# Finished weights and transposed rows as plane and exponential buffers, row-by-row guards, a reordered prologue and a new order of work in an attention and token-MLP kernel

## The chip, the cores and the metric

The kernel runs on one core of a Trainium2 chip. The core has a matrix engine (TensorE, PE in the profile, with its weight loads as PEld), a vector engine (VectorE, DVE), an activation engine (ScalarE, ACT), a general engine (GpSimd, POOL) and a queue engine (SyncE, SP) from which most transfers are issued. The metric is the device time of one execution in microseconds, as the median of several runs.

## The reference

For an input `x` of 2048 rows and 512 columns in bf16:

```python
xn = _layernorm(x)
def _A_ref(x, wqkv, wo):                     # 32 heads of 16 columns
    qkv = (x @ wqkv).reshape(B, S, 3, H, Dh)...
    p = _softmax(einsum("bhqd,bhkd->bhqk", q, k) * Dh ** -0.5)
    return einsum("bhqk,bhkd->bhqd", p, v)... @ wo
def _B_ref(x, w1, b1, w2, b2):               # an MLP over the rows, F = 1376
    h = _layernorm(x)
    u = _gelu(einsum("bsd,sf->bdf", h, w1) + b1)
    return (einsum("bdf,fs->bds", u, w2) + b2)...
return x + _A_ref(xn, ...) + _B_ref(xn, ...)
```

There are 32 heads x 2048 x 2048 exponentials to take, which is by far the largest part of the elementwise work.

## The kernel before

**Score tiles.** Attention is cut into 32 blocks: four groups of 512 queries (`qb`), each with eight groups of four heads. Within a block four heads sit in four rows (`r`, 32 partitions each) of PE, and the keys are cut into 16 tiles of 128 (`kt`). One unit is a tile of 128 keys by 512 queries for one head: 64 units a block, 2048 in all. The position in the order of work, `pos()`, is counted in blocks of 64 units. A score matmul (`score_mm`, L629) writes a unit into one of seven PSUM banks; the eighth collects P times V (`pv_mm`, L655).

**Two ways to an exponential.** An "A" unit is taken by ACT (`exp_tile`, L642): one, two or three banks in one instruction, written into the ring `pT` of `NU` = 16 slots, and then one PV matmul. A "D" unit is taken by VectorE (`dve_first`, L675): it adds a bias, clips and rounds the score to int16, whose bits read as bf16 are a piecewise linear power of two. Two more such numbers, shifted by constants, correct it. Four D units lie side by side in one plane of 2048 columns, and `make_plane` (L684, an addition of a constant to packed 64-bit integers on POOL; L686 on VectorE) makes the two shifted planes from the first. Each of the three is multiplied by V (the first by a scaled copy, `V17b`), so a D unit takes three PV matmuls.

**Planes.** `planes` holds `NXP` = 5 of them. The memory of `x_sb` gives four more once all 16 row tiles are normalized, that of `xn_sb` four more once the first MLP layer (`ut`) is done: `free_planes` (L1242). In those eight, each write of a row (L675) or of a whole plane (L684) also writes the keys of the old tenant (`plane_alias`), so the planner sees two writes to different rows of such a plane as writes of the same memory and puts a wait between them.

**Order of work.** The program is written out by a planner that runs while the kernel is built: `Sched` keeps each engine's stream, durations and dependences and turns a dependence on another operation into a semaphore wait. A prologue (L702 to L735) is in a fixed order: statistics, logarithm and exponential for the inverse deviation (`ln_rstd`, L508 and L510, on ACT), normalization (L515), transposes on PE (L554), copies out of PSUM (L566 and L567), the first Q and K, and the masked Q of the first two blocks (L593 and L595). After that a loop picks, for the engine that is free first, the best of what is ready: `burst` chooses how many of up to four scores go to ACT and how many to VectorE, and "chains" (K, V and Q projections, the MLP's two layers, output projection, epilogues) fill PE between them. Some 36 settings steer the choice; `STEP_VALUES` has one row of them for each block of 64 units. Those that matter below are `d_from` (position from which D units may be taken), `bal` and `bal_w` (tolerance for VectorE ending after ACT and the weight of what is over it) and `d_keep` and `d_last` (the last key tiles that are kept for ACT).

**Weights.** `wqkv_sb` holds the Q, K and V weights with 1536 columns for each of four slices of the contraction, and `xnT` the transposed normalized rows, 2048 columns for each slice. K and V of all heads are made in the first blocks, Q of a group of heads just ahead of its block. `w2blk` takes two blocks of the second MLP weights; `chain_late` loads the first two of them soon after the first block, though the second layer begins near position 15.7.

Of the kernel before, what the change touches and what calls it, by code (L numbers as in the profile page):

```python
# [41 lines left out]
def _plane_sum(i):  # L42
# [15 lines left out]
NXP = 5  # L58
DEBUG_CHAINS = False
# [1822 lines left out]
```

## Time and profile before

| | us |
|---|---|
| median of 3 runs | 688.4 (687.91 to 689.09) |
| profiled execution | 683.5 |
| its span, first to last instruction | 681.7 |
| ACT busy | 665.6 |
| PE busy | 661.3 |
| DVE busy | 572.3 |
| POOL busy | 481.5 |

The granted TensorE clock was 1.00 throughout. A group of instructions in the profile is one source line with one pair of tiles; its columns are the count, the busy time, the mean duration of one in nanoseconds, and the idle time of the engine ahead of the group with what ended it. Durations of neighbours on one engine can overlap, so the sum over a group may be above the time that the engine was occupied. A window of the trace lists for each engine the busy time and the number of instructions.

### The profile page before, as it was taken

The page shows a single profiled execution, that of the slowest core. Times are in us where ns is not written, and L with a number is a line of the kernel's source. Part 1 is how long each engine was busy: PE and PEld are TensorE (multiplying, and loading weights), DVE is VectorE, ACT ScalarE, POOL GpSimd, SP SyncE. Part 2 cuts the span into 40 slices and gives each one's busy share as a digit, 9 for nine tenths or more (in the row PEclk, how much of TensorE's full clock was granted, in tenths as well). Part 3 has the DMA queues.
Part 4 walks back from the last instruction along what each step waited for, and adds up shares of the span by engine and source line. Part 5 has one row for each costly group of instructions (what it writes and reads, how often), then busy time and mean ns, then how long its engine had stood idle before and what let it go on. Part 6 is the DMA issues. An engine that isn't in the chain of part 4 may idle for free.

```text
span 681.7 us, 20346 instructions
## 1 busy us (share of the span) xinstructions
PE 661.3 (97%) x8598; PEld 202.1 (30%) x8598; DVE 572.3 (84%) x937; ACT 665.6 (98%) x810; POOL 481.5 (71%) x506
## 2 busy tenths in 40 slices
PE   8899999999999999999999999999999999999997
PEld 3444433222222222222222222222222223222322
DVE  7987887778978888888898888888889888988875
ACT  6999999999999999999999999999999999999995
POOL 2407677887656866576896885776867898887783
PEclk9999999999999999999999999999999999999999
DMA  7033000201112111220103202121122112111001
GB/s 216 4 63 92 19 19 8 61 19 33 48 41 57 36 32 34 45 45 5 32 11 76 54 26 64 31 75 34 28 54 58 41 25 62 39 45 43 19 19 47
DMA packets 69956, 29.99 MB, mean 44 GB/s; under 512 B 56494, under 2 KB 66734, under 8 KB 69866
## 3 DMA queue, kind: packets, MB, share of 16 engines
q1 hardware_dynamic: 69290, 28.18, 16.9%
q8 instruction: 67, 1.10, 0.7%
q10 hardware_dynamic: 576, 0.52, 0.2%
q14 instruction: 23, 0.19, 0.1%
HBM read 22.15 MB, written 2.61 MB: 36 GB/s over the span
## 4 chain that ended last, share of the span: by engine, by line
ACT 82%; PE 12%; DVE 3%; POOL 2%; issue 1%; POOLq 0%; DVEq 0%; ACTq 0%
ACT pT L642 80%; PE ps L629 4%; PE ps L655 4%; PE ps L542 3%; POOL planes L684 1%; DVE x_sb L675 1%; ACT xres L968 1%; PE ps L548 1%; POOL x_sb L684 1%; POOL xn_sb L684 0%; ACT mv L510 0%; DVE xn_sb L515 0%; POOLq L335 0%; ACT mv L508 0%; DVE V17b L616 0%
## 5 line engine op out<-in xcount | busy, mean ns | idle before, releaser
L642 ACT ACTIVATE pT<-ps 128x1024 bf16<-128x1024 f32 (+2 forms) x770 | 653.9, 1098 | 1.0 <-PE ps L629 1.0
L629 PE MATMUL ps<-QT,KT 32*128 32x512 bf16 x2048 | 273.7, 385 | 9.3 <-ACT pT L642 4.6
L675 DVE TENSOR_SCALAR planes<-ps 128x512 int16<-128x512 f32 x289 | 193.0, 686 | 36.6 <-PE ps L629 35.6
L655 PE MATMUL ps<-pT,V 128*32 128x512 bf16 x1407 | 217.9, 387 | 1.1 <-DVE V L567 0.5
L675 DVE TENSOR_SCALAR x_sb<-ps 128x512 int16<-128x512 f32 x202 | 138.0, 687 | 29.3 <-PE ps L629 23.9
L629 PEld LDWEIGHTS ps<-QT,KT 32*128 32x128 bf16 x2048 | 75.0, 91 | 274.2 <-ACT pT L642 230.1
L684 POOL INT64_ADD planes<-x_sb x83 | 87.4, 1062 | 44.9 <-DVE x_sb L675 37.1
L675 DVE TENSOR_SCALAR xn_sb<-ps 128x512 int16<-128x512 f32 x150 | 102.4, 687 | 19.6 <-PE ps L629 15.0
L684 POOL INT64_ADD x_sb<-planes x87 | 90.7, 1047 | 33.3 <-DVE planes L675 20.8
L655 PE MATMUL ps<-planes,V 128*32 128x512 bf16 x562 | 111.4, 385 | 0.6 <-POOL planes L684 0.6
L684 POOL INT64_ADD planes<-planes x82 | 89.0, 1089 | 20.3 <-DVE planes L675 15.7
L655 PE MATMUL ps<-x_sb,V 128*32 128x512 bf16 x522 | 101.5, 385 | 0.0
L684 POOL INT64_ADD x_sb<-x_sb x51 | 56.0, 1101 | 38.9 <-DVE x_sb L675 34.9
L655 PE MATMUL ps<-planes,V17b 128*32 128x512 bf16 x289 | 78.0, 385 | 0.0
L655 PEld LDWEIGHTS ps<-pT,V 128*32 128x32 bf16 x1407 | 53.8, 94 | 68.5 <-issue 57.3
L542 PE MATMUL ps<-gT,w2blk 128*32 128x512 bf16 (+1 forms) x704 | 61.4, 383 | 0.0
L542 PE MATMUL ps<-xn_sb,w1blk 128*32 128x512 bf16 x688 | 57.7, 383 | 0.3 <-DVE qraw L875 0.3
L655 PE MATMUL ps<-x_sb,V17b 128*32 128x512 bf16 x202 | 51.1, 385 | 0.2 <-DVE OT L1096 0.2
L684 POOL INT64_ADD x_sb<-xn_sb x41 | 42.4, 1037 | 12.4 <-DVE xn_sb L675 7.4
L684 POOL INT64_ADD planes<-xn_sb x37 | 39.0, 1059 | 10.3 <-DVE xn_sb L675 7.1
L542 PE MATMUL ps<-xnT,wqkv_sb 128*32 128x512 bf16 (+3 forms) x624 | 43.3, 344 | 2.6 <-DVE xnT L567 1.7
L655 PE MATMUL ps<-xn_sb,V 128*32 128x512 bf16 x198 | 43.9, 385 | 0.0
(86 smaller groups left out, 558.3 us busy)
## 6 DMA issues: line engine op xcount, KB each, us to landing
w1blk<-in_B_w_dram SPq DMA_DIRECT2D x10, 512.0 KB, 4.9
w2blk<-in_B_w_dram SPq DMA_DIRECT2D x16, 320.0 KB, 3.4
denb<-rec_scr SPq DMA_DIRECT2D x16, 256.0 KB
xres<-in_A_x_dram SPq DMA_DIRECT2D x16, 128.0 KB, 3.7
QT<-qraw SPq DMA_DIRECT2D x120, 16.0 KB, 2.4
OT<-OT SPq DMA_DIRECT2D x60, 32.0 KB, 2.0
out_dram<-osb SPq DMA_DIRECT2D x13, 128.0 KB, 1.7
x_sb<-in_A_x_dram SPq DMA_DIRECT2D x2, 512.0 KB
```

The lines of the kernel that those rows point to most:

```text
L542: op = sc.add("pe", lambda e, sl=sl, c=c: e.matmul(dst[sl, :], lhsT=lhsT[:, sl], rhs=rhs, start=start, stop=stop, tile_position=(0, 32 * c ...
L548: return sc.add("pe", lambda e: e.matmul(bank(bk)[:, 0:n], lhsT=zer[:, 512:640], rhs=zer[:, 0:n], start=True, stop=True), reads=[("zer",)] ...
L629: return sc.add("pe", lambda e: e.matmul(bank(bk), lhsT=KT[32 * r:32 * r + 32, T, 128 * kt:128 * (kt + 1)], rhs=QT[32 * r:32 * r + 32, slo ...
L642: return sc.add("act", lambda e: e.activation(pick(pT, us), pick(ps3, bs), ACTF.Exp, scale=EXP_SCALE), reads=[("bank", b) for b in bs], wr ...
L655: return sc.add("pe", lambda e: e.matmul(bank(PV_BANK)[32 * r:32 * r + 32, :], lhsT=vt_[:, off:off + 32], rhs=rhs, start=start, stop=stop, ...
L675: return vec("dve", lambda e: e.tensor_scalar(plane_i[pb][:, 512 * r:512 * (r + 1)], bank(bk), BIAS + SHIFT[0], float(SHIFT[0]), ALU.add, ...
L684: return sc.add("pool", lambda e: e.int64_add(plane_q[pb], plane_q[pb0], -down * LANES), reads=rd, writes=wr, name="plane", occ=1015.0, la ...
L968: return sc.add("act", lambda e: e.activation(gB[0:m, :], gB[0:m, :], ACTF.Tanh, scale=2.0 * GELU_C * GC), reads=kB, writes=kB, occ=t["occ ...
```

## The change

1. **Regions.** `wqkv_sb` is laid out anew with each of the Q, K and V weights in one piece of 2048 columns (`wqkv4`), and `xnT` with each group of 512 rows in one piece (`xnT4`). Planes can now also lie in the first 2048 columns of `w2blk` (until position 14.2), in the V weights (once all K and V are made) and in the transposed rows of the query groups 0 to 2 (once, besides, that group's Q is made). The K weights' piece becomes four more ring slots for exponentials. The x planes come free one by one as four row tiles are normalized.
2. **Guards.** The first use of a region waits for the last operations on its old tenant (`last_ops`, kept in `old_ops`), as extra dependences; a write into a plane now writes the keys of its rows only.
3. **w2.** The first w2 blocks are loaded by a chain of their own from position 14.2, after the last operations on the plane that lay there. A memset of that plane joins the late constants.
4. **Prologue.** Statistics and inverse deviations of tiles 2 and 3 move ahead of copies of earlier tiles, two filling matmuls go, the copy of tile 2 goes to VectorE, the last 128 columns of the first Q go to bank 3, and the masked copies of Q are made in parts of 384 and 128 columns.
5. **Settings.** All 32 rows of `STEP_VALUES` have new numbers.

```diff
+RING_W = 1
+W2_POS = 14.2
...
-    (200.0, 2000.0, 10, 0, 1.2, 4, 4, 60, 0, 6, 0.0, 0, 3.0, 1.0, -0.1, 0.1, 2, 0.2, 2, 0.2, 1500, 2, 60.0, True, 1, False, 5, 4, 0, 1.5, 1000.0, 5, 6, 100.0, False, 3300.0),
...
+    (0.0, 2000.0, 8, 0, 0.8, 4, 2, 60, 0, 4, 400.0, 1, 3.0, 1.0, 0.1, 0.2, 2, 0, 2, 0.1, 800, 2, 100.0, True, 3, False, 5, 3, 0, 1.5, 1400.0, 6, 8, 0.0, False, 3300.0),
...
+        xnT4 = xnT_flat[:, :].rearrange("p (b ct n) -> p b ct n", b=NQB, ct=NCT)
+        wqkv4 = wqkv_flat[:, :].rearrange("p (j ct n) -> p j ct n", j=3, ct=NCT)
...
+            z += [lambda: memset("pool", w2_flat.bitcast(F32)[:, 0:1024], 0.0, [("pl", P_W2, r) for r in range(4)], 900)]
...
+        def qt_evac_part(e_, src, c0, c1, bk, key, eng):
+            rd, wr = [("bank", bk)] + [("qmask", e_, r) for r in range(4)], key
+            if eng == "act":
+                return vec("act", lambda e: e.activation(QT[:, e_, c0:c1], src, ACTF.Identity, scale=qmask[:, e_:e_ + 1]),
+                           rd, wr, c1 - c0)
...
+        regions += [(f, 2048 * j, [(nm, 4 * j + q) for q in range(4)]) for f, nm in ((x_flat, "x"), (xn_flat, "xn"))
+                    for j in range(4)]
+        P_X, P_XN, P_W2 = NXP, NXP + 4, NXP + 8
+        regions.append((w2_flat, 0, []))
+        P_W = len(regions)
+        regions += [(wqkv_flat, 2048 * (1 + j), [("wqkv", 1 + j, T) for T in range(4)]) for j in range(2) if j >= RING_W]
+        P_XT = len(regions)
+        regions += [(xnT_flat, 2048 * qb, [("xnT", 4 * qb + q) for q in range(4)]) for qb in range(3)]
...
+        U_X = NU + 1
+        N_UX = 4 * RING_W
+        pT_x = wqkv_flat[:, 2048:6144].rearrange("p (u n) -> p u n", n=512)
...
+        def region_deps(pb):
+            if regions[pb][2] and pb not in old_ops:
+                old_ops[pb] = last_ops(regions[pb][2])
+            return old_ops.get(pb, ())
...
-                       [("bank", bk)], [("pl", pb, r)] + plane_alias[pb], 512, name="p1")
+                          reads=[("bank", bk)], writes=[("pl", pb, r)], name="p1", extra_deps=region_deps(pb), **T_DVE(512))
...
-            wr = [("pl", pb, r) for r in range(4)] + plane_alias[pb]
+            wr = [("pl", pb, r) for r in range(4)]
...
         zeros(N_ZERO1)
         ln_rstd(1, 2)
+        ln_stats(2)
+        ln_rstd(2, 3)
         transpose_copy(0, 1, TBK[0], "act")
-        ln_stats(2)
         ln_norm(1)
         transpose_pe(1, TBK[1], 0)
         const_v(0, 1)
         pro_q(0)
-        zeros(N_ZERO2)
-        ln_rstd(2, 3)
+        ln_stats(3)
+        ln_rstd(3, 4)
         transpose_copy(1, 1, TBK[1], "act")
-        ln_stats(3)
         ln_norm(2)
         transpose_pe(2, TBK[2], 0)
-        pro_q(1)
-        ln_rstd(3, 4)
-        transpose_copy(2, 1, TBK[2], "act")
+        for ct in range(NCT):
+            kt_mm(0, 0, 1, ct, 2)
         ln_norm(3)
         transpose_pe(3, TBK[3], 0)
+        pro_q(1)
+        transpose_copy(2, 1, TBK[2], "dve")
+        kt_evac(0, 0, 1, 2, "act")
         pro_q(2)
-        for ct in range(NCT):
-            kt_mm(0, 0, 1, ct, 2)
         transpose_copy(3, 1, TBK[3], "dve")
-        kt_evac(0, 0, 1, 2, "act")
-        pro_q(3)
-        qt_evac_masked(0, 0, 0, 4, "dve")
-        qt_evac_masked(0, 0, 1, 4, "act")
+        pro_evac(0, 0, "act")
+        pro_q3()
+        pro_evac(0, 1, "dve")
+        pro_evac(1, 0, "act")
+        pro_evac(1, 1, "dve")
...
+            ch.steps = [Step("sp", yt_next, 600, gate=lambda: pos() >= W2_POS and P_W2 not in pl_busy) for _ in range(NW2)]
...
         def free_planes():
-            lim = list(range(NXP))
-            if nrm_done[0] == NT:
-                lim += list(range(NXP, NXP + 4))
+            lim = list(range(NXP)) + [P_X + j for j in range(4) if nrm_done[0] >= 4 * j + 4]
             if ut_done[0] == NFT:
-                lim += list(range(NXP + 4, NXP + 8))
+                lim += list(range(P_XN, P_XN + 4))
+            if consts_ok[0] and pos() < W2_POS:
+                lim.append(P_W2)
+            if kv_done():
+                lim += list(range(P_W, P_XT)) + [P_XT + q for q in range(3) if q_done[q] == 4]
             return [j for j in lim if j not in pl_busy]
```

More of the change, by code (lines that the diff above doesn't have):

```diff
@@ L574, in kt_mm @@
         def kt_mm(T, t0_, n_, ct, bk, off=0):
-            return mm_full(bank(bk)[:, off:off + 128 * n_], wqkv_sb[:, ct, D + 128 * T: D + 128 * T + 128],
-                           xnT[:, ct, 128 * t0_:128 * (t0_ + n_)], 128, 128 * n_, ct == 0, ct == NCT - 1,
+            return mm_full(bank(bk)[:, off:off + 128 * n_], wqkv4[:, 1, ct, 128 * T: 128 * T + 128],
+                           xnT4[:, t0_ // 4, ct, 128 * (t0_ % 4):128 * (t0_ % 4 + n_)], 128, 128 * n_, ct == 0, ct == NCT - 1,
                            [("wqkv", 1, T)] + [("xnT", t) for t in range(t0_, t0_ + n_)], bk)
@@ L584, in qt_mm @@
             t0_ = 4 * qb + c0 // 128
-            return mm_full(bank(bk)[:, c0:c0 + n], wqkv_sb[:, ct, 128 * T:128 * (T + 1)],
-                           xnT[:, ct, 512 * qb + c0:512 * qb + c0 + n], 128, n, ct == 0, ct == NCT - 1,
+            return mm_full(bank(bk)[:, c0:c0 + n], wqkv4[:, 0, ct, 128 * T:128 * (T + 1)],
+                           xnT4[:, qb, ct, c0:c0 + n], 128, n, ct == 0, ct == NCT - 1,
                            [("wqkv", 0, T)] + [("xnT", t) for t in range(t0_, t0_ + n // 128)], bk)
@@ L596, in qt_evac_masked @@
                        rd, wr, 565)
+        def qt_evac_part(e_, src, c0, c1, bk, key, eng):
[3 more added lines that the diff above has]
+                           rd, wr, c1 - c0)
+            return vec("dve", lambda e: e.tensor_scalar(QT[:, e_, c0:c1], src, qmask[:, e_:e_ + 1], None, ALU.mult),
+                       rd, wr, c1 - c0 + 50)
         def v_mm(t, T0_, T1_, ct, bk, off=0):
             n = 128 * (T1_ - T0_)
-            return mm_full(bank(bk)[:, off:off + n], xnT[:, ct, 128 * t:128 * (t + 1)],
-                           wqkv_sb[:, ct, 2 * D + 128 * T0_:2 * D + 128 * T1_], 128, n, ct == 0, ct == NCT - 1,
+            return mm_full(bank(bk)[:, off:off + n], xnT4[:, t // 4, ct, 128 * (t % 4):128 * (t % 4 + 1)],
+                           wqkv4[:, 2, ct, 128 * T0_:128 * T1_], 128, n, ct == 0, ct == NCT - 1,
                            [("wqkv", 2, T) for T in range(T0_, T1_)] + [("xnT", t)], bk)
@@ L632, in score_mm @@
                 tile_position=(32 * r, 0)),
-                reads=[("KTt", T, kt), ("QT", slot_q, r)], writes=[("bank", bk)], name="sc", cfg="S", n=512, last=last)
+                reads=[("KTt", T, kt), ("QT", slot_q, r)] + ([("QTp", b)] if b < 2 else []), writes=[("bank", bk)], name="sc", cfg="S", n=512, last=last)
         ps3 = ps[:, :].rearrange("p (b n) -> p b n", n=512)
@@ L641, in pick @@
                 return t3[:, v[0]:v[0] + w, :] if w > 1 else t3[:, v[0], :]
-            return sc.add("act", lambda e: e.activation(pick(pT, us), pick(ps3, bs), ACTF.Exp, scale=EXP_SCALE),
-                          reads=[("bank", b) for b in bs], writes=[("pT", u) for u in us], name="exp",
+            return sc.add("act", lambda e: e.activation(slots(us), pick(ps3, bs), ACTF.Exp, scale=EXP_SCALE),
+                          reads=[("bank", b) for b in bs], writes=[("pT", u) for u in us], name="exp", extra_deps=slot_deps(us),
                           occ=427.0 * w + 50.0, lat=427.0 * w + 248.0)
@@ new lines, in bass_parallel_sum__softmax_full_mha__mixer_token_mlp__prompt_kernel, with last_ops @@
+        plane_i = [f.bitcast(I16)[:, o:o + 2048] for f, o, _ in regions]
+        plane_b = [f[:, o:o + 2048] for f, o, _ in regions]
+        plane_q = [f.bitcast(I64)[:, o // 4:o // 4 + 512] for f, o, _ in regions]
+        U_X = NU + 1
+        N_UX = 4 * RING_W
+        pT_x = wqkv_flat[:, 2048:6144].rearrange("p (u n) -> p u n", n=512)
+        old_ops = {}
+        def last_ops(keys):
+            z = {}
+            for k in keys:
+                for o in [sc.last_writer.get(k)] + list(sc.readers.get(k, ())):
+                    if o is not None:
+                        q = ("d", id(o)) if o.is_dma else o.eng
+                        if q not in z or o.pos > z[q].pos:
+                            z[q] = o
+            return list(z.values())
@@ new lines, in region_deps, with slot_deps, slots @@
+        def region_deps(pb):
+            if regions[pb][2] and pb not in old_ops:
+                old_ops[pb] = last_ops(regions[pb][2])
+            return old_ops.get(pb, ())
+        def slot_deps(us):
+            if us[0] >= U_X:
+                if "ring" not in old_ops:
+                    old_ops["ring"] = last_ops([("wqkv", 1 + j, T) for j in range(RING_W) for T in range(4)])
+                return old_ops["ring"]
+            return ()
+        def slots(us):
+            t3, a = (pT_x, us[0] - U_X) if us[0] >= U_X else (pT, us[0])
+            return t3[:, a:a + len(us), :] if len(us) > 1 else t3[:, a, :]
@@ L681, in make_plane @@
             rd = [("pl", pb0, r) for r in range(4)]
[L682 removed]
+            wr = [("pl", pb, r) for r in range(4)]
             if eng == "pool":
                 return sc.add("pool", lambda e: e.int64_add(plane_q[pb], plane_q[pb0], -down * LANES),
[L685 to L687 removed]
+                              reads=rd, writes=wr, name="plane", occ=1015.0, lat=1130.0, port=True, extra_deps=region_deps(pb))
+            return sc.add("dve", lambda e: e.tensor_scalar(plane_i[pb], plane_i[pb0], -float(down), None, ALU.add),
+                          reads=rd, writes=wr, name="plane", port=True, extra_deps=region_deps(pb), **T_DVE(2048, 4.0))
         for i in range(N_ZERO0):
@@ L700, in zeros, with pro_q3, pro_evac @@
                 zero_mm(7)
+        def pro_q3():
+            for ct in range(NCT):
+                mm_full(bank(3)[:, 0:128], wqkv4[:, 0, ct, 0:128], xnT4[:, 0, ct, 384:512], 128, 128, ct == 0, ct == NCT - 1,
+                        [("wqkv", 0, 0), ("xnT", 3)], 3)
+        def pro_evac(e_, c, eng):
+            if c == 0:
+                return qt_evac_part(e_, bank(4)[:, 0:384], 0, 384, 4, [("QTp", e_)], eng)
+            return qt_evac_part(e_, bank(3)[:, 0:128], 384, 512, 3, [("QT", e_, r) for r in range(4)], eng)
         const_q()
@@ L920, in chain_late @@
             steps += [ld_wo] + [lambda e_=e_, r=r: ld_wop(e_, r) for e_ in range(2) for r in range(4)]
-            steps += [lambda: yt_next() for _ in range(NW2)]
             ch = Chain("late", [], 90.0, 0.0, ex=False)
@@ L1286, in ring_pick @@
         def ring_pick(w, taken=()):
-            v = {u: sc.ready(writes=[("pT", u)]) for u in range(NU) if ring_free[u] and u not in taken}
+            v = {u: sc.ready(writes=[("pT", u)]) for u in range(len(ring_free)) if ring_free[u] and u not in taken}
             z = runs_of(v, w)
@@ L1492, in rel @@
                         ring_free[uu] = True
-                    items[u[0]][r].append(dict(t=ex.end, k="A", kt=u[1], rhs=pT[:, uu, :], key=("pT", uu), which=0, rel=rel))
+                    items[u[0]][r].append(dict(t=ex.end, k="A", kt=u[1], rhs=slots((uu,)), key=("pT", uu), which=0, rel=rel))
         def issue_d(ds, i, n):
```

60 lines of the change are left out of this document (32 added, 28 removed), and 62 rows, old and new, of the table STEP_VALUES.

## The prediction

> **What bounds the kernel now.** I read the page's busy shares first, then its chain of work that ended last, then who waited for whom, then the costliest groups.
>
> ```profile
> PE 661.3 (97%) x8598; PEld 202.1 (30%) x8598; DVE 572.3 (84%) x937; ACT 665.6 (98%) x810; POOL 481.5 (71%) x506
> ...
> ACT 82%; PE 12%; DVE 3%; POOL 2%; issue 1%; POOLq 0%; DVEq 0%; ACTq 0%
> ...
> L642 ACT ACTIVATE pT<-ps 128x1024 bf16<-128x1024 f32 (+2 forms) x770 | 653.9, 1098 | 1.0 <-PE ps L629 1.0
> ```
>
> Two engines look full, PE and ACT. The chain is 82% ACT, and the exponentials (L642) sat idle for only 1.0 us. The waits of the whole run say which of the two leads:
>
> ```profile
> PEld ps L629 <- ACT pT L642: 230.1, 535, 0.9
> ```
>
> PE waits for ACT 535 times, 230 us in all (a score cannot start until an exponential has emptied its PSUM bank); ACT's 1.0 us of waiting, in the row above, is its whole wait for PE. So the end is set by ACT's exponentials. The exception is a stretch in which the chain in order of time leaves ACT:
>
> ```profile
> 70.17 0.40 PE ps L629 x4
> ...
> 79.15 0.33 PE ps L655 x4
> ...
> 80.06 0.55 PE ps L655 x8
> ...
> 141.24 0.34 PE ps L629 x2
> 141.60 15.56 ACT pT L642 x15
> ```
>
> From 70 to 141 us it runs mostly on PE. Eight PV matmuls take 0.55 us and four 0.33, so four more cost 0.22, one 0.055.
>
> There are 2048 score tiles of 128x512, and each goes one of two ways: to ACT ("A": one exponential, one PV matmul) or to VectorE ("D": one L675, its share of the plane additions on POOL, three PV matmuls). The whole kernel is one ledger: start to first exponential, the A tiles, tail. So I need the price of an A tile and the D share by stage, from the windows 100 to 340 us (MLP's first layer and gelu running, xn_sb not yet a plane) and 340 to 655 us (xn_sb free). Busy time of all engines, then of L675 alone, then the groups of exponentials in the one window and in the other:
>
> ```profile
> 100.00:340.00 240.00, 236.18 (x2844) 67.53 (x2836) 202.37 (x307) 239.78 (x268) 171.82 (x163) 1.00 0.16 35
> 340.00:655.00 315.00, 312.44 (x3824) 87.00 (x3821) 270.96 (x419) 314.73 (x374) 249.58 (x242) 1.00 0.17 43
> ```
> ```profile
> 100.00:340.00 240.00, 153.44 (x228) 1.00 0.16 35
> 340.00:655.00 315.00, 238.77 (x360) 1.00 0.17 43
> ```
> ```profile
> L642 ACT ACTIVATE pT<-ps 128x1024 bf16<-128x1024 f32 x210 | 204.5, 1216 | 0.2 <-PE ps L629 0.2
> L642 ACT ACTIVATE pT<-ps 128x1536 bf16<-128x1536 f32 x22 | 33.3, 1539 | 0.0
> L642 ACT ACTIVATE pT<-ps 128x512 bf16<-128x512 f32 x25 | 18.6, 819 | 0.0
> ```
> ```profile
> L642 ACT ACTIVATE pT<-ps 128x1024 bf16<-128x1024 f32 x309 | 291.8, 1176 | 0.3 <-PE ps L629 0.2
> L642 ACT ACTIVATE pT<-ps 128x512 bf16<-128x512 f32 x64 | 40.1, 739 | 0.0
> ```
>
> Second window: 618 + 64 = 682 A tiles in 315 us in which ACT did little else, 0.46 us each (durations overlap, so I divide the window). It had 360 D tiles, 34.5% of 1042. First window: 420 + 66 + 25 = 511 A and 228 D, 30.9%. **One tile moved from ACT to VectorE is worth 0.46 us as long as ACT leads.** VectorE is busy 202.4/240 = 84% in the first window and 271/315 = 86% in the second.
>
> **The change part by part.** *Prologue.* ACT and then VectorE in the timeline, 7 to 12 us:
>
> ```profile
> 7.08 0.29 ACT L508 ACTIVATE mv<-mv,epsb 128x1 f32<-128x1 f32 x1
> ...
> 10.09 0.28 ACT L566 ACTIVATE KT<-ps 128x128 bf16<-128x128 f32 x1 [0.95 <-PE ps L542]
> 11.30 0.69 ACT L593 ACTIVATE QT<-ps,qmask 128x512 bf16<-128x512 f32 x1 [0.93 <-DVE QT L595]
> 11.88 0.59 ACT L642 ACTIVATE pT<-ps 128x512 bf16<-128x512 f32 x1
> ```
> ```profile
> 7.02 0.18 DVE L503 BATCH_NORM_AGGREGATE mv<-stats 128x2 f32<-128x6 f32 x1
> ...
> 8.61 0.41 DVE L515 TENSOR_SCALAR xn_sb<-x_sb,mv 128x512 bf16<-128x512 bf16 x1 [0.56 <-ACT mv L510]
> ...
> 10.45 0.75 DVE L595 TENSOR_SCALAR QT<-ps,qmask 128x512 bf16<-128x512 f32 x1 [0.52 <-PE ps L542]
> ```
>
> Tile 3 is normalized (L515, 8.61) behind a wait for ACT, whose logarithms for tiles 2 and 3 stand behind copies of earlier tiles. With logarithm and square root issued ahead of those copies, tile 3's statistics (done at 7.20) pass ACT in about 0.55 us, and its normalization starts near 7.8: 0.8 us earlier. VectorE's order up to there is unchanged, so no load need be earlier. Then the last quarter of Q goes to a bank of its own and VectorE scales 128 columns instead of 512: unseen, between ACT's 0.28 for 128 columns and VectorE's own 0.75; I take 0.3, saving 0.45. ACT scales the other 384 columns twice (between 0.28 and 0.69 each, say 0.55) beside PE's last quarter; its own queue (copy, K, two Q parts) then ends about when the first score does, near 10.6, and is late next. **-1.2 us**, bounds 0 (the following K tiles come no earlier) and -1.3.
>
> *Planes sooner, and more of them.* The first D tile, and the memsets that must precede it:
>
> ```profile
> 45.83 0.69 DVE L675 TENSOR_SCALAR x_sb<-ps 128x512 int16<-128x512 f32 x1
> ```
> ```profile
> 24.57 4.88 POOL L414 MEMSET planes<- 128x1024 f32 x5
> ```
>
> The settings let D begin at 0.8 of a block's 64 tiles; before, row 0 says 1.2 and row 1 (from tile 64) 0.8, so in fact 1.0. That frees 13 tiles; at one in three about 4 become D. The sixth memset costs POOL 4.88/5 = 0.98 us near 30 us, 15 us before it matters. VectorE has layer-norm work there that the planner ranks lower, so I take 3: **-1.4 us**; bounds 0 and -1.8. PE pays 2 x 0.055 = 0.11 us per D tile.
>
> From 100 to 340 us the planner has 9 planes; it gets the w2 block until 14.2 blocks, the V weights once K and V are done, and the transposed rows of finished query blocks: 12, later 13. In the second window it already had 13 and VectorE was only two points busier. If VectorE rises to that 86%, n more D tiles (0.6 us each back to back, below) satisfy 202.4 + 0.6n = 0.86(240 - 0.46n): n = 4. The busiest 20 us of the run bound it above:
>
> ```profile
> 600.00:620.00 20.00, 20.00 (x259) 5.55 (x251) 18.16 (x30) 20.00 (x24) 15.88 (x16) 1.00 0.23 59
> ```
>
> At 18.16/20 = 91%, n = 15. I take 6, near the row that holds for 315 us rather than for 20: **-2.8 us**, bounds 0 and -7.
>
> *Row guards.* In the old code a first write into an x_sb or xn_sb plane also counts as a write of the whole old region, so two rows of one plane wait for each other; in the `planes` tensor they do not. VectorE's timeline near the end:
>
> ```profile
> 658.96 1.28 DVE L675 TENSOR_SCALAR planes<-ps 128x512 int16<-128x512 f32 x2
> 660.16 1.48 DVE L675 TENSOR_SCALAR xn_sb<-ps 128x512 int16<-128x512 f32 x2
> ```
>
> With 0.69 for the last of each, the spacing is 0.59 against 0.79: 0.2 us for each adjoining pair. The groups give the total:
>
> ```profile
> L675 DVE TENSOR_SCALAR planes<-ps 128x512 int16<-128x512 f32 x289 | 193.0, 686 | 36.6 <-PE ps L629 35.6
> ...
> L675 DVE TENSOR_SCALAR x_sb<-ps 128x512 int16<-128x512 f32 x202 | 138.0, 687 | 29.3 <-PE ps L629 23.9
> ...
> L675 DVE TENSOR_SCALAR xn_sb<-ps 128x512 int16<-128x512 f32 x150 | 102.4, 687 | 19.6 <-PE ps L629 15.0
> ```
>
> Idle not put down to PE is 5.4 + 4.6 us against 1.0 for `planes`: about 9 us of VectorE. It is off the path, so worth nothing itself; turned wholly into D tiles it would be 15 x 0.46 = 7 us. After 340 us, where most of it lies and three or four buffers and four exponential slots are also added, I take 3 tiles: **-1.4 us**, bounds 0 and -7.
>
> *At nothing.* The relaid wqkv and xnT keep their column runs, so their matmuls, copies and loads keep their sizes. The two w2 loads move from about 57 us to 14.2 blocks, some 320 us in:
>
> ```profile
> 57.31 1.11 SPq L406 DMA_DIRECT2D w2blk<-in_B_w_dram  x2
> 58.46 0.29 SPq L406 DMA_DIRECT2D w2blk<-in_B_b_dram  x1
> ```
>
> That is six issues, 2.9 us of SP's queue, now waiting for the last readers of that plane. Behind them stand spreads of Q and stores; the spreads are due 1.5 blocks (30 us) ahead, and the first use of w2 is as far off. If a reader were late by a plane's life of some microseconds, that lead covers it.
>
> The Trainium skill, page "SBUF — State Buffer", section "Who interferes with whom", speaks against more D tiles: a VectorE instruction with two SBUF inputs and a GpSimd one that reads SBUF share a port, and one blocks for the other's whole length. The trace agrees:
>
> ```profile
> L959 DVE TENSOR_TENSOR osb<-gT 128x512 f32<-128x512 bf16 (+1 forms) x11 | 11.8, 1076 | 0.1
> ...
> L1096 DVE COPY OT<-ps 128x512 f32<-128x512 f32 x11 | 7.5, 682 | 0.1
> ```
>
> The gelu square takes 1076 ns beside 682 for a copy of that size out of PSUM. Six more D tiles lengthen POOL's 172 us by some 4, 2.5% of an excess of 11 x 0.4 us: 0.1 us. By the rule the sum is -6.7, without it -6.8.
>
> **Sum.** -1.2 - 1.4 - 2.8 - 1.4 = -6.8 us, 12 more D tiles being 5.6 of it. The span goes from 681.7 to 674.9, the profiled execution (683.5, 1.8 around the span) to 676.7. That execution lies 4.9 below the median of the three timed runs (688.4); I apply the difference to the median: **681.6 us**.
>
> **The rivals.** *(a) The new buffers lie idle.* For: VectorE is 84% busy with 9 planes and 86% with 13, so something else (one D tile beside each pair of A tiles, seven PSUM banks) may cap it. Against: the wait between rows is real. Then only prologue and early start are left, -1.2 to -2.6: 686.5. *(b) PE takes over.* Each D tile adds 0.11 us to PE, and between 70 and 141 us PE leads already. Against: in the whole run PE has 230 us of waiting for ACT, so 12 tiles (1.3 us) meet no wall outside that stretch. If half the D gain falls there: -1.2 - 2.8 = -4.0: 684.4. *(c) Slower: the new settings send fewer tiles to VectorE.* The tolerance for VectorE ending after ACT (`bal`) falls from 200 to 0 in the first seven rows and from 900 to 600 in the next ones, which pushes tiles back to ACT at 0.46 us each. For: nothing but the unseen plan stands against it. Against: more planes allow more open groups. With the prologue's -1.2, it decides from 6 fewer D tiles (2.6/0.46), below 635 of now 641; at 12 fewer the time is 688.4 - 1.2 + 5.5 = 692.7.
>
> **How the numbers follow.** Forecast (gain over 4.5 us) 0.66, (a) 0.14, (b) 0.10, (c) 0.10. Faster and slower are told apart from no change at 0.2%, 1.4 us. (a) reaches into "same" with half its chance: faster 0.83, same 0.07, slower 0.10. The range runs from 675.0 (13.4 less: prologue 1.2, early start at its bound of 1.8, and 10.4 of the 14 that bound the other two) to 688.0, leaving out (c) and a little below 675.
>
> **What would show it.** The last exponentials before:
>
> ```profile
> 669.44 4.03 ACT L642 ACTIVATE pT<-ps 128x512 bf16<-128x512 f32 x5
> ```
>
> They end at 673.5, which leaves a tail of 8.2 us. Expected after: first exponential near 10.7 us; first L675 near 40; more than 641 of them, about 653, with the gain in 100 to 340 us; L675 on w2blk, wqkv_sb and xnT; adjoining xn_sb pairs at 1.28 us, not 1.48; w2 loads at 320 us. Wrong: 641 or fewer L675 (a, c); ACT idle before L642 beyond a few us (b); or a tail longer than 8.2 us.

## The result and the profile after

| | before | after |
|---|---|---|
| median of 4 runs | 688.43 (687.91 to 689.09) | 676.13 (675.75 to 677.11) |
| ratio, 95% interval | | 0.9823 (0.9806 to 0.9840) |
| profiled execution, its span | 683.5, 681.7 | 677.1, 675.3 |
| ACT busy | 665.6 | 655.6 |

The change makes the kernel 12.3 us faster, 1.8%. First the page of after: busy time of each engine, the chain that ended last, and the exponentials, which are now L658 and go to the ring `pT` or to the four slots in the memory of the K weights (`wqkv_sb`).

```profile
PE 652.9 (97%) x8608; PEld 202.0 (30%) x8608; DVE 582.0 (86%) x964; ACT 655.6 (97%) x809; POOL 502.6 (74%) x522
...
ACT 84%; PE 11%; DVE 4%; DMA 0%; issue 0%; DVEq 0%
...
L658 ACT ACTIVATE pT<-ps 128x1024 bf16<-128x1024 f32 (+2 forms) x652 | 561.8, 1053 | 4.9 <-PE ps L645 4.6
...
L658 ACT ACTIVATE wqkv_sb<-ps 128x1024 bf16<-128x1024 f32 (+2 forms) x117 | 128.5, 1134 | 0.5 <-PE ps L645 0.5
```

The bound is the same as before: 84% of the chain is ACT. It does 10 us less work, and it waits 5.4 us ahead of its exponentials where the first profile of before had 1.0.

Then the groups of VectorE's first writes (now L721) by the memory that they write: count, least, median and greatest duration, the start of the first and of the last.

```profile
L721 DVE TENSOR_SCALAR planes<-ps x232: 621/681/693, 56.2 to 657.1; 128x512 int16<-128x512 f32 x116
L721 DVE TENSOR_SCALAR x_sb<-ps x182: 627/681/693, 44.1 to 653.4; 128x512 int16<-128x512 f32 x182
L721 DVE TENSOR_SCALAR xn_sb<-ps x102: 628/684/693, 335.2 to 660.7; 128x512 int16<-128x512 f32 x102
L721 DVE TENSOR_SCALAR xnT<-ps x96: 628/681/693, 154.7 to 659.5; 128x512 int16<-128x512 f32 x96
L721 DVE TENSOR_SCALAR wqkv_sb<-ps x33: 674/682/692, 168.9 to 646.9; 128x512 int16<-128x512 f32 x33
L721 DVE TENSOR_SCALAR w2blk<-ps x20: 673/680/692, 70.8 to 293.4; 128x512 int16<-128x512 f32 x20
```

The counts add up to 665 D tiles, 24 more than the 641 of before, and 149 of them (96 + 33 + 20) lie in memory that was not a plane before. The column of first starts tells from when each region is used: w2's block from 71 us, the transposed rows from 155 and the V weights from 169 us, once K and V are done.

The windows in which the prediction worked, for all engines and then for L721 alone:

```profile
100.00:340.00 240.00, 236.51 (x2928) 67.36 (x2926) 213.49 (x328) 239.46 (x279) 197.06 (x181) 1.00 0.17 38
340.00:655.00 315.00, 311.68 (x3880) 89.37 (x3877) 271.53 (x433) 314.92 (x377) 253.00 (x246) 1.00 0.17 44
```
```profile
0.00:100.00 100.00, 24.49 (x37) 0.97 0.24 63
100.00:340.00 240.00, 158.53 (x245) 1.00 0.17 38
340.00:655.00 315.00, 240.26 (x375) 1.00 0.17 44
```

Against before the first window has 17 more D tiles (245 for 228), the second 15 more (375 for 360), the start one fewer (37 for 38) and the end seven fewer (8 for 15), since the kernel now reaches it earlier. VectorE rose from 84% to 89% in the first window (213.5 of 240 us). In the second it stayed at 86%, 271.5 us busy for 271.0, with 15 more tiles: there it is not busier, but does more of the work that counts.

### The profile page after: what moved, and what is told of

It reads as the page before. It is cut to its first block, busy times and chain, and to the rows that moved or that the text cites. A ratio compares the mean times of both kernels' runs of the same rounds, so it can differ in the third digit from the quotient of the medians.

```text
span 675.3 us, 20208 instructions
## 1 busy us (share of the span) xinstructions
PE 652.9 (97%) x8608; PEld 202.0 (30%) x8608; DVE 582.0 (86%) x964; ACT 655.6 (97%) x809; POOL 502.6 (74%) x522
## 4 chain that ended last, share of the span: by engine, by line
ACT 84%; PE 11%; DVE 4%; DMA 0%; issue 0%; DVEq 0%
ACT pT L658 69%; ACT wqkv_sb L658 14%; PE ps L645 4%; PE ps L671 3%; PE ps L549 3%; DVE xn_sb L522 1%; ACT xres L1033 1%; DVE x_sb L721 1%; DVE stats L508 0%; DMA x_sb<-in_A_x_dram 0%; PE ps L561 0%; DVE osb L1024 0%; DVE V L574 0%; ACT L1033 0%; PE ps L1698 0%
## 5 line engine op out<-in xcount | busy, mean ns | idle before, releaser
L658 ACT ACTIVATE pT<-ps 128x1024 bf16<-128x1024 f32 (+2 forms) x652 | 561.8, 1053 | 4.9 <-PE ps L645 4.6
L671 PE MATMUL ps<-pT,V 128*32 128x512 bf16 x1156 | 192.4, 388 | 4.5 <-DVE V L574 4.5
L721 DVE TENSOR_SCALAR planes<-ps 128x512 int16<-128x512 f32 x232 | 153.3, 684 | 25.8 <-PE ps L645 25.3
L721 DVE TENSOR_SCALAR x_sb<-ps 128x512 int16<-128x512 f32 x182 | 120.0, 683 | 14.2 <-PE ps L645 13.6
L658 ACT ACTIVATE wqkv_sb<-ps 128x1024 bf16<-128x1024 f32 (+2 forms) x117 | 128.5, 1134 | 0.5 <-PE ps L645 0.5
L671 PE MATMUL ps<-wqkv_sb,V 128*32 128x512 bf16 x318 | 83.7, 386 | 0.0
L730 POOL INT64_ADD x_sb<-planes x62 | 64.9, 1051 | 21.8 <-DVE planes L721 11.3
L721 DVE TENSOR_SCALAR xn_sb<-ps 128x512 int16<-128x512 f32 x102 | 68.2, 684 | 12.2 <-PE ps L645 11.9
L730 POOL INT64_ADD planes<-x_sb x58 | 62.8, 1088 | 13.9 <-DVE x_sb L721 12.1
L721 DVE TENSOR_SCALAR xnT<-ps 128x512 int16<-128x512 f32 x96 | 63.9, 684 | 9.1 <-PE ps L645 8.8
L730 POOL INT64_ADD planes<-planes x50 | 55.2, 1107 | 7.6 <-DVE planes L721 7.6
```

Source lines behind the costliest of these rows:

```text
L658: return sc.add("act", lambda e: e.activation(slots(us), pick(ps3, bs), ACTF.Exp, scale=EXP_SCALE), reads=[("bank", b) for b in bs], write ...
L671: return sc.add("pe", lambda e: e.matmul(bank(PV_BANK)[32 * r:32 * r + 32, :], lhsT=vt_[:, off:off + 32], rhs=rhs, start=start, stop=stop, ...
L721: return sc.add("dve", lambda e: e.tensor_scalar(plane_i[pb][:, 512 * r:512 * (r + 1)], bank(bk), BIAS + SHIFT[0], float(SHIFT[0]), ALU.ad ...
L730: return sc.add("pool", lambda e: e.int64_add(plane_q[pb], plane_q[pb0], -down * LANES), reads=rd, writes=wr, name="plane", occ=1015.0, la ...
```

## The experiments

Three things were open. The same program of before took 683.5 us in its profile and 688.4 in its timed runs; after waits 5.4 us ahead of its exponentials; and 24 tiles came where 12 were expected, with nothing to tell memory, guards and settings apart. My theory for the first two was that the late memsets on POOL hold VectorE up; for the third that the 9 us of waits between rows, put down as worth little, carry a good part of the gain. The rivals: the 5 us is something that differs all along between executions; and the memory or the settings alone would bring the gain.

**The kernel before once more** (no edit).

> The kernel before, unchanged, to see where its profiled execution (683.5 us) and the median of its timed ones (688.4 us) differ. Theory 1 (the memsets on POOL hold up a normalization L515 on VectorE, by chance 1 us in the profile and 4 to 6 us in most executions): a new profile of about 688 us has a pair of L515 near 27 us that takes 4 us or more instead of 1.6, and ACT idle there. Rival (the clock or the chip): the new profile has the same L515 pair at 1.6 us and is longer everywhere, with a clock below 1.00. Time 688.4 us within 1.

It took 688.17 us (ratio to the other runs of before 0.9999, 0.9990 to 1.0009), and now the profile too is of such an execution, with a span of 686.1. Its timelines on POOL, VectorE and ACT (start, duration, instruction, and in brackets the idle time ahead of it):

```profile
24.08 4.51 POOL L414 MEMSET planes<- 128x1024 f32 x5
28.52 0.20 POOL L414 MEMSET b1r<- 11x128 bf16 x1
28.67 0.95 POOL L414 MEMSET wo_pad<- 128x1024 bf16 x1
```
```profile
25.34 4.37 DVE L616 TENSOR_SCALAR V17b<-V 128x272 bf16<-128x272 bf16 x1
29.62 0.62 DVE L567 COPY xnT<-ps 128x1024 bf16<-128x1024 bf16 x1
```
```profile
31.27 1.57 ACT L642 ACTIVATE pT<-ps 128x512 bf16<-128x512 f32 x3 [3.75 <-PE ps L629]
33.76 1.02 ACT L642 ACTIVATE pT<-ps 128x1024 bf16<-128x1024 f32 x1 [0.91 <-PE ps L629]
```

The scaling of V, 128x272 from SBUF to SBUF, takes 4.37 us and ends as the row of memsets ends (28.67 + 0.95 = 29.62); in the first profile of before it took 0.67. The copy behind it feeds PE, PE feeds ACT, and ACT waits 3.75 and 0.91 us. The place and the sum were expected; the victim was the scaling, not the pair of normalizations.

One sign of the rival appeared too, a clock below 1.00 (0.993 in the mean), but only here: PE ran no matmul from 26 to 30 us, and its granted clock, 1.00 until 28 us, was 0.50 from 30 to 34 us and 1.00 again from 36. The other sign, longer everywhere, did not. Up to the 20th exponential this execution is 0.5 us ahead of the first profile, from the 24th to the last it is 4.3 to 4.4 us behind, so all of the loss arises between them. How much of it is waiting for VectorE and how much the halved clock behind it was not separated; the next run removes both.

**Memsets that let VectorE go first.** The order is kept in both kernels; each memset of the late constants also waits for the last VectorE operation ahead of it in the plan that the kernel marks with `port` (normalizations, scalings of V and the like, from SBUF to SBUF):

```diff
+        last = None
+        for o in sc.order:
+            if o.eng == "dve" and o.port:
+                last = o
+            elif o.eng == "pool" and o.port and o.name == "" and last is not None and last not in o.deps:
+                o.deps.append(last)
         sc.plan()
```

> The kernel before with the same order on every engine; each memset on POOL also waits for the last normalization or other 2x/4x-mode operation on VectorE that stands ahead of it in the planned order. Theory 1: about 684 us, 4 to 5 below the kernel before, and no L515 above 1 us. Rival (the gap between profile and timed runs is elsewhere): 688.4 us, no change.

> The changed kernel with the same order on every engine and the same extra waits of memsets. In its trace a pair of normalizations (L522) takes 4.13 us behind the six plane memsets, and ACT then idles 5.4 us ahead of exponentials instead of 1.0. Theory (the memsets are the cause and ACT's idle time is on the path): 672 us, 4 below the changed kernel, L522 pair at about 0.75 us, idle ahead of exponentials about 1 us. Rival (the K and V projections of that stage are late anyway, PE or VectorE takes the place of the memsets): 675 to 676 us and the idle time stays.

Before with this edit takes 682.96 us (0.9923, 0.9908 to 0.9938): 5.4 us gone, where 4 to 5 were expected. Its POOL and VectorE:

```profile
25.57 0.95 POOL L415 MEMSET planes<- 128x1024 f32 x1 [0.56 <-DVE V17b L617]
26.73 0.95 POOL L415 MEMSET planes<- 128x1024 f32 x1 [0.20 <-DVE xn_sb L516]
```
```profile
25.31 0.20 DVE L617 TENSOR_SCALAR V17b<-V 128x272 bf16<-128x272 bf16 x1
25.43 0.69 DVE L568 COPY xnT<-ps 128x1024 bf16<-128x1024 bf16 x1
26.14 1.68 DVE L516 TENSOR_SCALAR xn_sb<-x_sb,mv 128x512 bf16<-128x512 bf16 x2
```

The scaling is down to 0.20 us, the memsets still end by 31 us, and nobody misses them. The granted clock from 20 to 40 us is 1.00, where the run before this one had 0.83. The span of 681.1 is within 0.6 us of that of the first profile of before.

After with this edit takes 674.19 us (0.9795, 0.9780 to 0.9810), 1.9 below after: the fastest version of this study, 14.2 us below before. That is about half of the 4 us that ACT had waited in this stretch, and it lies between the theory's 672 and the rival's 675 to 676. After's own VectorE and POOL, and then ACT and VectorE with the edit:

```profile
26.95 4.13 DVE L522 TENSOR_SCALAR xn_sb<-x_sb,mv 128x512 bf16<-128x512 bf16 x2 [0.33 <-ACT mv L517]
```
```profile
24.18 4.52 POOL L420 MEMSET planes<- 128x1024 f32 x5
28.63 0.96 POOL L420 MEMSET w2blk<- 128x1024 f32 x1
```
```profile
26.58 5.36 ACT L659 ACTIVATE pT<-ps 128x1024 bf16<-128x1024 f32 x8 [0.51 <-PE ps L646]
31.76 0.35 ACT L516 ACTIVATE mv<-mv,epsb 128x2 f32<-128x2 f32 x1
32.14 0.21 ACT L518 ACTIVATE mv<-mv 128x2 f32<-128x2 f32 x1
...
36.55 1.51 ACT L659 ACTIVATE pT<-ps 128x512 bf16<-128x512 f32 x2 [1.42 <-PE ps L646]
```
```profile
32.38 0.41 DVE L523 TENSOR_SCALAR xn_sb<-x_sb,mv 128x512 bf16<-128x512 bf16 x1 [2.03 <-ACT mv L518]
```

The edit frees the normalizations (4.13 us to 1.57), but the next ones wait 2.03 us for an inverse deviation whose logarithm stands behind eight exponentials in ACT's queue (5.36 us), and ACT then waits 1.42 us for the scores that follow. This second wait belongs to the order of after: before, with the same edit, has six exponentials (3.87 us) ahead of that logarithm, and no such wait.

**The old waits between rows, put back into after.** Same order, same tiles; only each write into a plane of `x_sb` or `xn_sb` waits again for the write into the same plane ahead of it:

```diff
+        last = {}
+        for o in sc.order:
+            if o.reg is not None and P_X <= o.reg < P_W2:
+                d = last.get(o.reg)
+                if d is not None and d not in o.deps:
+                    o.deps.append(d)
+                last[o.reg] = o
         sc.plan()
```

> The changed kernel with the same order on every engine; only the old waits between writes into one plane of x_sb or xn_sb are put back. Theory (VectorE is off the path, the waits cost it 0.2 us for each adjoining pair, some 6 us in all, and ACT hardly notices): 676 to 677.5 us, adjoining xn_sb pairs back at 1.48 us. Rival (a late first write holds a PSUM bank, so PE and ACT get it late): 679 us or more, with more idle time ahead of exponentials.

683.46 us (0.9928, 0.9911 to 0.9944), 7.3 above after: more than half of the whole gain, as the rival had it and not the theory. Of its page, then from the view of L722 alone how long PE's weight loads waited for it (us, times), and the same of L721 in after:

```profile
PE 44%; ACT 41%; DVE 12%; issue 1%; DMA 0%; DVEq 0%
...
L659 ACT ACTIVATE pT<-ps 128x1024 bf16<-128x1024 f32 (+2 forms) x652 | 559.5, 1013 | 8.1 <-PE ps L646 6.5
...
L722 DVE TENSOR_SCALAR x_sb<-ps 128x512 int16<-128x512 f32 x182 | 123.7, 685 | 18.3 <-PE ps L646 12.3
```
```profile
  PEld ps L646: 20.6, 58
```
```profile
  PEld ps L645: 13.4, 35
```

VectorE's idle ahead of `x_sb` writes that is not PE's doing is 6.0 us again (18.3 - 12.3). PE waits 58 times, 20.6 us, for a first write to empty a bank, where in after it waited 35 times, 13.4 us. That 7.2 us more is about what the kernel loses. The chain that ended last, 84% ACT in after, is now 41% ACT and 44% PE. A pair of first writes into `xn_sb` in this run, and one in after:

```profile
400.10 1.47 DVE L722 TENSOR_SCALAR xn_sb<-ps 128x512 int16<-128x512 f32 x2
```
```profile
660.10 1.33 DVE L721 TENSOR_SCALAR xn_sb<-ps 128x512 int16<-128x512 f32 x2
```

The loss builds up over the whole run: the 100th exponential starts 0.3 us later than in after, the 300th 1.8, the 500th 3.9 and the last 7.2. So I read it as the small waits on VectorE reaching PE, and then ACT. The rows agree with that, but no run tests that path by itself, and the edit makes POOL's additions into these planes wait as well.

**The same waits taken away from before.** On top of the memset edit; again the order is kept:

```diff
+        for o in sc.order:
+            if o.reg is not None and o.reg[0] >= NXP:
+                o.deps = [d for d in o.deps if d.reg is None or d.reg[0] != o.reg[0] or d.reg[1] == o.reg[1]]
```

> The kernel before with the memset waits of the run before_port (682.96 us) and the same order on every engine; the waits between first writes into different rows of one x_sb or xn_sb plane are taken away (each row is still written after its own readers). Theory A (a late first write holds its PSUM bank, so PE and ACT get it late; putting such waits into the changed kernel cost 7.3 us with 284 writes, here there are 352): 675 to 678 us. Theory B (this order of work was planned with the waits in it, so they cost little where it knew of them): 681 to 683 us. Adjoining xn_sb pairs fall to 1.28 us in both.

682.96 us (0.9918, 0.9901 to 0.9936), to the hundredth the time with the waits, as theory B had it. Two rows of its page:

```profile
L677 DVE TENSOR_SCALAR planes<-ps 128x512 int16<-128x512 f32 x289 | 193.8, 686 | 41.3 <-PE ps L631 40.1
...
L677 DVE TENSOR_SCALAR x_sb<-ps 128x512 int16<-128x512 f32 x202 | 135.4, 686 | 27.6 <-PE ps L631 26.4
```

The idle not due to PE fell here from 5.6 us to 1.2, and the wait of `planes` for PE rose from 35.5 to 40.1: VectorE arrives earlier and waits longer for the next score. PE's wait for its first writes hardly moves:

```profile
  PEld ps L630: 9.1, 23
```
```profile
  PEld ps L631: 7.9, 19
```

(with the waits, then without). In that order ACT idled only 1.0 us ahead of its exponentials with the waits and 1.1 without, so there was nothing for it to gain. The two runs together show that the same kind of wait costs nothing in an order that was planned with it and 7.3 us in one that was planned without it. That the planner of after filled the freed time with tiles is my reading, and not shown: no run plans the new memory with the old waits in place, or the old memory without them.

**One part of the change at a time.** Settings and memory crossed: after with the 32 rows of settings of before; after whose w2 block, V weights and transposed rows never become planes; and before with the 32 new rows.

```diff
-            if consts_ok[0] and pos() < W2_POS:
-                lim.append(P_W2)
-            if kv_done():
-                lim += list(range(P_W, P_XT)) + [P_XT + q for q in range(3) if q_done[q] == 4]
+            kv_done()
```

> The changed kernel with the 32 rows of settings of the kernel before; regions, guards and prologue as changed. Its order of work has 629 first writes on VectorE instead of 665. Ledger (0.465 us for each tile that goes back to ACT): 676.1 + 36 x 0.465 = 692.9 us, slower than the kernel before. Rival (the memory and the guards bring the gain, the settings are only fine tuning): 676 to 682 us.

> The changed kernel in which w2, V weights and transposed rows are never used as planes; ring slots, guards, prologue and settings as changed. Its order of work has 600 first writes on VectorE instead of 665. Ledger: 676.1 + 65 x 0.465 = 706.3 us. Rival (VectorE or PE, not the count of tiles, sets the end, so it falls by less): 690 us or less.

> The kernel before with the 32 new rows of settings and nothing else. Its order of work has 598 first writes on VectorE instead of 641. Ledger: 688.4 + 43 x 0.465 = 708.4 us. Rival (the new settings are better by themselves): 684 us or less.

| run | us | ratio to before | D tiles | ACT busy | ACT idle ahead of exponentials to the ring |
|---|---|---|---|---|---|
| before (memsets in the way) | 688.17 | 0.9999 | 641 | 666.0 | 5.7 |
| after | 676.13 | 0.9823 | 665 | 655.6 | 4.9 |
| after, old settings | 703.50 | 1.0218 (1.0193 to 1.0244) | 629 | 674.9 | 11.6 |
| after, new planes unused | 710.24 | 1.0316 (1.0292 to 1.0340) | 600 | 688.6 | 5.9 |
| before, new settings | 721.40 | 1.0478 (1.0442 to 1.0515) | 598 | 693.3 | 8.9 |

All three are slower than the kernel before. The direction in ACT's busy time follows the count of tiles, as the ledger wants, but the times lie 4 to 13 us above what counting tiles gave, so there is a loss that no count shows. In the run with the old settings the first 100 us hold most of it: of the 11.6 us of idle time ahead of exponentials 10.9 lie there (4.8 in after), beside a scaling of V that took 6.27 us next to the memsets and a granted clock of 0.61 to 0.71 between 30 and 60 us. In the other two its source was not looked for; that an order not fitted to its memory has more waits is a guess. Settings and memory are fitted to each other, so "what the settings bring" has no answer of its own. With the old rows the rest of the change (memory, guards, prologue) costs 15.1 us (703.5 against 688.4); with the new rows it gains 45.3 (721.4 against 676.1).

**Memory with a settings row that is fitted to neither.** One row for all 32 blocks, the same in both kernels: row a from after's table, row b from before's.

```diff
-    (200.0, 2000.0, 10, 0, 1.2, 4, 4, 60, 0, 6, 0.0, 0, 3.0, 1.0, -0.1, 0.1, 2, 0.2, 2, 0.2, 1500, 2, 60.0, True, 1, False, 5, 4, 0, 1.5, 1000.0, 5, 6, 100.0, False, 3300.0),
...
+    (600.0, 2000.0, 8, 0, 0.8, 3, 2, 200, 20, 6, 0.0, 0, 1.5, 1.5, 0.6, 9.0, 99, 0.2, 2, 0.1, 1500, 2, 150.0, True, 2, True, 4, 2, 0, 1.5, 2000.0, 4, 6, 150.0, False, 3300.0),
...
```

The fence shows the first of 32 rows taken out and the first of 32 equal rows put in, for row a in the kernel before.

> The kernel before with one row of settings (the new table's row for block 9) for all blocks, so tuned to neither kernel. 638 first writes on VectorE. Ledger alone: 688.4 + 3 x 0.465 = 689.8 us; the two kernels with foreign settings (703.5 and 721.4 us) lay 10 to 13 us above their ledgers, so 700 to 703.

> The changed kernel (regions, guards, prologue) with the same one row for all blocks. 644 first writes. Theory (memory and guards are worth something under any settings, as more tiles on VectorE): below flat_a_before by 6 x 0.465 + 0.8 of prologue = 3.6 us. Rival 1 (the gain lies in the tuned rows alone): equal within 1 us. Rival 2 (more buffers also spare ACT idle time, which the count of tiles does not show): more than 8 us below.

> The kernel before with one row of its own table (block 28) for all blocks. 620 first writes on VectorE. Ledger alone 688.4 + 21 x 0.465 = 698.2 us; with 10 to 13 us on top as in the other untuned kernels, 708 to 711.

> The changed kernel with that same row for all blocks. 636 first writes. Theory: below flat_b_before by 16 x 0.465 + 0.8 = 8.2 us. Rival 1: equal within 1 us. Rival 2: more than 14 us below.

| row | before | after | difference | ACT busy | span less ACT busy |
|---|---|---|---|---|---|
| a | 714.63 | 697.64 | -17.0 | 676.3 to 671.4 | 35.9 to 25.0 |
| b | 721.28 | 700.88 | -20.4 | 688.5 to 677.7 | 30.1 to 21.0 |

Memory, guards and prologue together gain 17 and 20 us, with only 6 (638 to 644) and 16 tiles (620 to 636) more on VectorE. My theory had 3.6 and 8.2 us, so rival 2 holds; and both versions of before came out 10 us and more above what I expected. The rest, 11 us of the 17 and 9 of the 20, is time in which ACT did nothing. The group of single exponentials of before with row a shows such time:

```profile
L642 ACT ACTIVATE pT<-ps 128x512 bf16<-128x512 f32 x340 | 205.6, 700 | 19.1 <-PE ps L629 15.1 <-PE ps L561 3.6
```

Of the 19.1 us ahead of these, 15.1 are waits for a score; the same group of after with row a waits 8.7 us. On the chip of these four runs the unedited kernel before took 683.56 us (683.44 to 683.61), as in its first profile: by the time, the 5 us of the memsets did not occur there. They are not wholly out of the comparison: with row a one normalization of before took 2.92 us beside the memsets, and 5.0 us of the saved idle time lie in the first 100 us (8.4 to 3.4), while with row b that stage goes the other way (0.9 to 5.9, with a pair of normalizations of 2.00 us in after).

## Why the prediction was right, and where its terms were wrong

It said 681.6 us in a range of 675.0 to 688.0, and faster; 676.13 is inside, near the low end. The ledger can be closed on two executions that both have the memsets in the way, before_again and after:

| term, us | predicted | measured | from |
|---|---|---|---|
| first exponential | -1.2 | -0.8 | 11.39 to 10.59 |
| ACT busy (D tiles: +12, then +24) | -5.6 | -10.4 | 666.0 to 655.6 |
| ACT idle ahead of exponentials | 0 | -0.3 | 5.7 to 5.4 |
| last exponential to end | 0 | +0.7 | 8.2 to 8.9 |
| sum, and the spans | -6.8 | -10.8 | 686.1 to 675.3 |

With the memset edit in both the same account reads -0.8, -10.4, +2.3 and -0.1, which makes the -9.0 between the spans of 681.1 and 672.1. So of the 12.3 us between the medians 8.8 (682.96 to 674.19) are the new memory, guards, order and prologue. The other 3.5 are a loss that both kernels have and that is smaller in after: 5.4 us in before, 1.9 in after. The prediction had carried that loss over unchanged, so these 3.5 us moved the result by luck, and on a chip where before takes 683.6 us after was not run. It was luck as well that the terms missed in both directions: next to nothing from the early start, and 32 tiles in the two windows instead of 9.

- **The bound, and 0.46 us for a tile: right.** ACT leads throughout, and 24 tiles took 10.4 us off it, 0.43 each.
- **Prologue, -1.2: right in mechanism, a third too large.** The first exponential came at 10.59 us, where it was expected at 10.6 to 10.7. Before itself begins 0.5 us earlier in its later profiles (11.39) than in the first one (11.88) from which the term was taken. In after's ACT timeline the first exponential follows 0.14 us behind the masked copies:

```profile
9.40 1.05 ACT L609 ACTIVATE QT<-ps,qmask 128x384 bf16<-128x384 f32 x2 [0.73 <-PE ps L549]
10.59 2.92 ACT L658 ACTIVATE pT<-ps 128x512 bf16<-128x512 f32 x4
```

- **Early start, -1.4: wrong.** The first L721 is at 44.11 us, not near 40, and the first 100 us hold 37 D tiles, not 41. The permission in the settings was read rightly, but the layer-norm and the memset ahead of it were held up. With the memset edit the first one starts at 41.66 us and there are 39. Before with that edit has its first at 45.30 us and 38 tiles, so like for like the start moved by 3.6 us and brought one tile.
- **100 to 340 us, -2.8: too small.** 17 tiles instead of 6, a little over the 15 that the busiest 20 us allowed. The new planes were counted rightly; the choice of a value near VectorE's 86% of later was not borne out: it went to 89%. (With the memset edit in both kernels the counts are 229 and 244 here, 361 and 377 in the second window: 15 and 16 more.)
- **Row guards and second window, -1.4: much too small.** 15 tiles instead of 3. The step that failed is the size of this term: the 9 us of VectorE were taken as "off the path, so worth nothing itself", with a small part turned into tiles. The number that came is that of the upper bound, all of it turned into 15 tiles, and VectorE's busy time in that window did not grow. How many of the 15 stand on the guards and how many on the new planes and the four ring slots is not shown. For the program of before the quoted words hold (no gain from taking the waits away); in the order of after they do not, where the waits cost 7.3 us.
- **At nothing: right for the w2 loads, wrong for the memset.** The loads now go out at 323 us and nothing waits for them:

```profile
323.31 1.25 SPq L411 DMA_DIRECT2D w2blk<-in_B_w_dram  x2
```

  The sixth memset was priced by its own length and by when it is needed. What mattered was what runs beside it: the memsets cost after 1.9 us through VectorE. What the sixth adds to that was not separated.
- **The base.** I took the profile's execution as the median's with 4.9 us spread over it. They were one stall at 25 us, which the profile that I read did not have, so no row of it could tell.
- **Rivals.** The new buffers don't lie idle (149 tiles in them). PE does not take over: ACT is busy 239.5 of the 240 us from 100 to 340. Fewer tiles to VectorE: no, 665, and 635 would have been the turning point; with only one half of the change that rival is what happens (629, 600 and 598 tiles, all slower). Its argument read `bal` in part only: in the last twelve rows all but one rise from 600 to 900, which is the other way.
- **Signs of being wrong.** Two that the prediction named did appear: 5.4 us of idle time ahead of exponentials, and a tail of 8.9 us. The first was not PE taking over, since before_again has 5.7 us; the memset edit takes it down to 3.3. The second is 8.0 us in the run with the edit, and what made it longer in this execution is not known.

Left open: what a plan with the old guards and the new memory would give; what the transposed rows, the V weights, the w2 block and the four ring slots bring each; what the prologue brings alone; and whether a plan that puts the logarithms ahead of the eight exponentials would take the last 2.3 us of after. These weren't run.

## What to carry to other kernels

In a kernel whose order a planner writes, what vanishes when a false dependence is taken out of the finished program is a poor price for it: such waits were worth 0 in one order and 7.3 us in the other. What the planner could put in their place is the better question, though no run here measured it by itself. Memory that is dead early is worth looking for as buffers, but the order must be fitted again with it: half of such a change was slower than none of it. When a profiled execution and the timed median differ by more than the runs scatter, take the profile again until they agree before subtracting anything from either.

## What the runs showed of the hardware that was not expected

A row of POOL memsets issued back to back held up a VectorE instruction from SBUF to SBUF for as long as the row lasted. The scaling of V took 4.37 us instead of 0.20 beside memsets of 0.9 us each, and a pair of normalizations 4.13 instead of 1.57. The Trainium skill, page "SBUF — State Buffer", section "Who interferes with whom", says of a VectorE instruction in a two-port mode and one of GpSimd that whoever issues first has the shared ports for the whole instruction and that the other is blocked fully. The blocking agrees; by that rule the loss would be, as an estimate from the trace's memsets, what is left of one, at most 0.9 us, and here it lasted from the second of the five `planes` memsets to the end of `wo_pad`, the last of the row. With a wait on VectorE's work added ahead of the memsets the loss of 5.4 us was gone in before and 1.9 us of it in after, although two and three memsets still ran back to back in those runs.

Whether it happens is not fixed by the program. On the chip of the first experiments every timed execution of before took 687.75 to 689.77 us, on that of the last four all three took 683.44 to 683.61. The first profile of before shows the same memsets with VectorE getting in between:

```profile
25.83 0.67 DVE L616 TENSOR_SCALAR V17b<-V 128x272 bf16<-128x272 bf16 x1
26.42 0.62 DVE L567 COPY xnT<-ps 128x1024 bf16<-128x1024 bf16 x1
26.96 1.60 DVE L515 TENSOR_SCALAR xn_sb<-x_sb,mv 128x512 bf16<-128x512 bf16 x2
```

There the five memsets took 4.88 us and not 4.51, so it was POOL that gave way, and that execution took 683.5 us. The scaling starts 1.26 us after the first of the memsets in both executions (25.83 - 24.57 and 25.34 - 24.08), so the two don't differ by that start; what decides between them stays open.
